# Sigmoid attention and a gated MLP on one core: in the first round the last keys' scores are placed ahead of the unit before's last values, with three smaller moves

## The chip, the core and the metric

The kernel runs on one core of a Trainium2 chip. The metric is the device time of one execution in microseconds (us); lower is better. The engines that matter here are TensorE (PE in the profile, its weight loads PEld), VectorE (DVE), ScalarE (ACT) and the queue that issues the transfers (SP). Each engine takes its instructions in the order in which the program has them; an instruction that has to wait for another engine holds back everything behind it on its own engine.

## What is computed

```python
scores = scale * np.matmul(q, k.transpose(0, 1, 3, 2)) - np.log(S)   # 8 batches, 12 heads, S = 448, head size 64
attn = 1.0 / (1.0 + np.exp(-scores))                                 # sigmoid, no row sum
x = heads side by side of np.matmul(attn, v)                         # (8, 448, 768)

h = np.maximum(x @ w_in, 0.0)                                        # (8, 448, 1024), halves u and v
v_n = (v - mean) / sqrt(var + 1e-6)                                  # over the features
v_s = einsum('ts,bsd->btd', w_spatial, v_n) + b_spatial
out = (u * v_s) @ w_out
```

All of it is in 32-bit numbers. Most products are made as three reduced-precision products of a high and a low part (`TERMS`, line 240): the high part of an operand is a rounded copy, the low part is what the copy left over. So an operand costs one cast and one subtraction before TensorE can use it.

## The kernel before

The eight batches go in four rounds of two. A round is attention for two batches, then the MLP for them: gate values (`pv`), the spatial product (`pg`), the other half (`pu`), the output (`po`). Rounds two to four use `attention` (lines 582 to 687). The first round has a routine of its own, `first_attention` (lines 528 to 580), since the weights are still being loaded and converted during it. The change is in that routine and in two helpers that it calls.

**A unit.** The first round has six units, n = 0, 2, 4, 6, 8, 10. Each holds two pairs of heads, `units[n]` and `units[n + 1]`. A pair's 448 keys are three full tiles of 128 and a rest of 64. The score tiles of a unit are numbered t: 0, 1, 2 are the full tiles of the first pair (`FIRST`), 4, 5, 6 those of the second (`SECOND`), and t = 3 is the short tile with the last 64 keys of both pairs. For each t, `attention_scores` (line 245) puts the scores of two heads into `psc`, a pair of PSUM banks, by six matmuls for a full tile (line 269) or by four plain 32-bit ones for the short tile (line 257; the profile counts each of these as two). ScalarE then writes the sigmoid into an SBUF buffer `at` (line 277). `attention_values` (line 284) multiplies the `at` tiles with the values and sums them over all seven t in one PSUM pair, `pav` (line 307). `attention_sums` (line 316) takes the finished `pav` out of PSUM as high and low parts of `x_s`: ScalarE casts the first head pair's half (line 319), VectorE casts the other half (line 320) and then makes both subtractions (line 322). In the profile's rows `qks` is a pair's split queries and keys, and `raw` what was loaded for it.

**Banks.** PSUM is used as four bank pairs, and `latest` holds them in the order of their last use. For each unit after the first they are named y, z, w, x (line 571). The short tile gets y, the full tiles get z, w, y, x, z, w, and `pav` gets y. Bank pair x still holds the `pav` of the unit before when a unit begins; t = 4, the fourth full tile, is the first to write into it. So t = 4 can begin only when all four instructions of `attention_sums` for the unit before have ended.

**Order of a unit (lines 571 to 579).** First `short_values(n - 2)`: the last products of the unit before, and its sums. Then `short_scores(n, y)`, then six full score tiles. Between some of these `load_weights(1)` runs one portion of the weight preparation (`weight_steps`, line 150). A portion is the integer part, the shift part or the split of one weight block, on VectorE; the first portion of a block also issues the transfer for the block two further on. Then come `splits(n + 2)`, a portion, `splits(n + 3)`: the high and low parts of the next unit's queries and keys, cast by ScalarE and subtracted by VectorE. Last come the products of the six full tiles. The short tile's products wait for the next unit.

**Buffers.** `at` tiles take their buffer from the list `big` of seven in turn (`slot`, line 113).

The profile's times below are of unit 2 (from 15.68 us), the others being alike.

Of the kernel before, what the change touches and what calls it, by code (L numbers as in the profile page):

```python
# [14 lines left out]
P = 128  # L15
# [20 lines left out]
def attn_gmlp_kernel(  # L36
# [25 lines left out]
    nc = tc.nc  # L62
# [9 lines left out]
    NFULL = 3  # L72

    FULL = NFULL * P
    GAP = 16
    REST = FULL + GAP
    PART = REST + S
# [28 lines left out]
    def split(hi, lo, src, copy):  # L106
        copy(hi, src)  # L107
        nc.vector.tensor_sub(lo, src, hi.bitcast(F32))  # L108

    tmp = [f"tmp_{i}" for i in range(3)]  # L110
    big = [f"big_{i}" for i in range(7)]

    def slot(tags, name, shape=(P, 2, 512), dtype=F32):
        tag = tags.pop(0)
        tags.append(tag)
        return work.tile(list(shape), dtype, tag=tag, name=name, bufs=1)

    def banks(name, tag=None):
        tag = tag or latest[0]
        latest.remove(tag)  # L120
        latest.append(tag)
        return sums.tile([P, 2, 512], F32, tag=tag, name=name)
# [71 lines left out]
    def load_weights(n):  # L194
        for _ in range(n):
            next(weights, None)
# [27 lines left out]
    def attention_splits(b, hp):  # L224
        raw = loaded[b, hp][:, HALF:]
        s = work.tile([P, 2, 2 * S], F32R, tag="split", name=f"qks_{b}_{hp}", bufs=3)
        if b == hp == 0:

            chunk, rest, query = slice(FULL - P, FULL), slice(0, FULL - P), slice(REST, PART)
            nc.vector.tensor_copy(s[:, 0, query], raw[:, query])  # L230
            for cols in (chunk, rest):
                nc.scalar.copy(s[:, 0, cols], raw[:, cols])
            for cols in (chunk, query, rest):
                nc.vector.tensor_sub(s[:, 1, cols], raw[:, cols], s[:, 0, cols].bitcast(F32))
        else:
            scalar = b == 1 or b == 0 and hp not in (1, 2)
            split(s[:, 0, :PART], s[:, 1, :PART], raw[:, :PART], nc.scalar.copy if scalar else nc.vector.tensor_copy)
        parts_of[b, hp] = s
# [6 lines left out]
    def attention_scores(b, hp, t, tag=None, slots=big, raws=None):  # L245

        psc = banks(f"psc_{b}_{hp}_{t}", tag)
        heads = [slice(j * D, (j + 1) * D) for j in range(2)]
        if t == NFULL:
            for odd in range(2):  # L250
                if raws is None:
                    raw = loaded[b, hp + odd]
                    key, query = raw[:, :HALF], raw[:, HALF + REST :]
                else:
                    key, query = raws[:, odd, :HALF], raws[:, odd, HALF:]
                for j, rows in enumerate(heads):
                    nc.tensor.matmul(  # L257
                        psc[odd * HALF : (odd + 1) * HALF, j, :S],
                        key[rows],
                        query[rows],  # L260
                        start=True,
                        stop=True,
                    )
        else:
            s = parts_of[b, hp + t // (NFULL + 1)]
            k = (t % (NFULL + 1) + NFULL - 1) % NFULL * P
            for i, (a, e) in enumerate(TERMS):
                for j, rows in enumerate(heads):
                    nc.tensor.matmul(  # L269
                        psc[:, j, :S],  # L270
                        s[rows, a, k : k + P],
                        s[rows, e, REST:PART],
                        start=i == 0,
                        stop=i == len(TERMS) - 1,
                    )
        at = slot(slots, f"at_{b}_{hp}_{t}")[:, :, :S]
        nc.scalar.activation(at, psc[:, :, :S], AF.Sigmoid, bias=bias_s, scale=QK)  # L277
        return at
# [5 lines left out]
    def attention_values(b, hp, t, at, tag=None, apart=False):  # L284

        key = b, hp, apart and t == NFULL
        if key not in pav_of:
            pav_of[key] = banks(f"pav_{b}_{hp}_{t}", tag)
            tag_of[key] = latest[-1]
        pav = pav_of[key]  # L290
        if t == NFULL and b > 1:
            latest.sort(key=lambda tag: tag == tag_of[key])
        vt = values[b, hp]
        for odd in range(2):
            if t == NFULL:
                rows = slice(odd * HALF, (odd + 1) * HALF)
            elif (t > NFULL) == odd:
                rows = slice(0, P)
            else:
                continue  # L300
            unit = key, odd
            count[unit] = count.get(unit, 0) + 1
            total = NFULL + 1 if not apart else 1 if t == NFULL else NFULL
            start, stop = count[unit] == 1, count[unit] == total
            for j in range(2):
                heads = slice(j * D, (j + 1) * D)
                nc.tensor.matmul(  # L307
                    pav[heads, odd, :S], vt[rows, t, heads], at[rows, j], start=start, stop=stop
                )
        return pav[:, :, :S]  # L310

    def x_parts(b, hp):
        x = x_s[:, :, hp : hp + 2, (b % 2) * S : (b % 2 + 1) * S]
        return x[:, 0], x[:, 1]

    def attention_sums(b, hp, pav):

        hi, lo = x_parts(b, hp)
        nc.scalar.copy(hi[:, 0], pav[:, 0])
        nc.vector.tensor_copy(hi[:, 1], pav[:, 1])  # L320
        for i in range(2):
            nc.vector.tensor_sub(lo[:, i], pav[:, i], hi[:, i].bitcast(F32))

    def product(ps, pairs, more=(), start=True, stop=True):
# [177 lines left out]
    units = [(b, hp) for b in range(B) for hp in range(NHP)]  # L502
# [21 lines left out]
    def loads(f, n, end=end):  # L524
        if n < end:
            f(*units[n])

    def first_attention():

        shorts = {}  # L530

        def splits(n):
            loads(attention_splits, n)

        def short_scores(n, tag):
            shorts[n] = attention_scores(*units[n], NFULL, tag)
            loads(attention_loads, n + 4)

        def short_values(n):
            pav = attention_values(*units[n], NFULL, shorts.pop(n))  # L540
            attention_sums(*units[n], pav)

        splits(0)
        for n in range(0, end, 2):
            unit = units[n]
            full = []

            def scores(t, tag=None):
                if n == 0 and t in (1, NFULL + 1):
                    splits(1 if t == 1 else 2)  # L550
                full.append((*unit, t, attention_scores(*unit, t, tag)))
                if t == 0:
                    loads(attention_loads, n + 3)
                    loads(value_loads, n + 2)
                if t > NFULL if n == 0 else t not in (2, TILES - 1):
                    load_weights(1)

            def products(tag=None):
                for args in full:
                    attention_values(*args, tag)  # L560

            if n == 0:
                for t in FIRST:
                    scores(t)
                short_scores(n, None)
                for t in SECOND:
                    scores(t)
                splits(3)
                products()
                continue  # L570
            y, z, w, x = latest
            short_values(n - 2)
            short_scores(n, y)
            for t, tag in zip((*FIRST, *SECOND), (z, w, y, x, z, w)):
                scores(t, tag)
            splits(n + 2)
            load_weights(1)
            splits(n + 3)
            products(y)
        short_values(end - 2)  # L580

    def attention(m):

# [11 lines left out]
        def splits(*ns):  # L595
            for n in ns:
                attention_splits(*units[first + n])
# [107 lines left out]
    for m in range(B // 2):  # L705
        if m == 0:
            first_attention()
        else:
            for _ in running:
                pass  # L710
# [87 lines left out]
```

## Time and profile before

| | |
|---|---|
| three runs | 670.29, 670.58, 670.66 us; median 670.58 us |
| the profiled execution | 670.48 us, of which the profile's span is 668.7 us |
| busy in the span | PE 664.5 us, DVE 331.2, ACT 224.8, POOL 19.4 |
| first round's attention | the span's start to 67.36 us |
| each later round | 164.6 us, of which attention 60.6 us in round two |

The span runs from the first to the last instruction that was recorded; the execution's own time has 1.8 us around it. Rows of the timeline give start, duration, engine, line, operation, tiles and shape, and in brackets the idle time of the engine before it with what ended that. Rows of the chain give start, duration and what the chain of the work that ended last went through. A weight load's (PEld) idle time shows when TensorE was held by another engine, since a matmul's recorded duration may cover a short wait.

### The profile page before, as it was taken

The numbers are of one execution on the slowest core, as the hardware profiler recorded it, in microseconds if no ns is written. First come the engines' busy times: TensorE is split into PE (matmuls) and PEld (weight loads), VectorE is DVE, ScalarE is ACT, GpSimd is POOL, SyncE is SP. The second block draws the span as 40 slices with busy tenths as digits, with TensorE's granted clock in tenths as the row PEclk, the third lists the DMA queues.
The fourth block names the chain that finished last, engine by engine and source line by source line (L and its number), as shares of the span: only waits on it lengthen the run. The fifth ranks groups of instructions, "written<-read, shape, count | busy, mean of one in ns | idle before, by whom it ended". The sixth has DMA issues, their size and how long they took to land.

```text
span 668.7 us, 9073 instructions
## 1 busy us (share of the span) xinstructions
PE 664.5 (99%) x3866; PEld 510.4 (76%) x3866; DVE 331.2 (50%) x501; ACT 224.8 (34%) x265; POOL 19.4 (3%) x36
## 2 busy tenths in 40 slices
PE   9999999999999999999999999999999999999998
PEld 5554889999655588999964558899985556899997
DVE  5999899841357447231145644722024554653201
ACT  6877010121567510002176731010128663101112
POOL 0000010000000002000000001100000000110000
PEclk9999999999999999999999999999999999999999
DMA  8783222331445300002153430000216410000022
GB/s 299 266 270 124 63 63 67 109 111 52 163 150 168 112 1 1 0 1 82 56 182 105 163 112 1 0 1 1 82 56 197 140 60 1 0 1 1 0 83 82
DMA packets 22328, 57.34 MB, mean 86 GB/s; under 512 B 2832, under 2 KB 10128, under 8 KB 22288
## 3 DMA queue, kind: packets, MB, share of 16 engines
q1 hardware_dynamic: 22288, 56.76, 25.1%
q8 instruction: 30, 0.49, 0.3%
q14 instruction: 10, 0.08, 0.0%
HBM read 45.74 MB, written 11.01 MB: 85 GB/s over the span
## 4 chain that ended last, share of the span: by engine, by line
PE 99%; DVE 0%; issue 0%
PE pav L307 20%; PE pv L328 17%; PE pu L328 17%; PE po L328 17%; PE psc L269 14%; PE pg L328 11%; PE psc L257 3%; PE idle L701 1%; PE po_end L328 0%; DVE osb L499 0%
## 5 line engine op out<-in xcount | busy, mean ns | idle before, releaser
L277 ACT ACTIVATE at<-psc,bias_s 128x896 f32<-128x896 f32 x168 | 154.3, 1017 | 44.8 <-PE psc L269 23.5
L307 PE MATMUL pav<-at,v 128*64 128x448 f32 (+1 forms) x768 | 134.6, 545 | 0.1
L328 PE MATMUL pu<-x_s,w_u_s 128*128 128x448 f32 x576 | 117.1, 362 | 0.0
L328 PE MATMUL po<-gs,w_out_s 128*128 128x448 f32 (+1 forms) x576 | 116.2, 361 | 0.0
L328 PE MATMUL pv<-w_v_s,x_s 128*128 128x512 f32 x504 | 115.5, 390 | 0.0
L328 PEld LDWEIGHTS pu<-x_s,w_u_s 128*128 128x128 f32 x576 | 108.0, 187 | 7.2
L328 PEld LDWEIGHTS po<-gs,w_out_s 128*128 128x128 f32 x576 | 107.6, 187 | 7.1
L328 PEld LDWEIGHTS pv<-w_v_s,x_s 128*128 128x128 f32 x504 | 94.3, 188 | 22.4 <-issue 2.8
L307 PEld LDWEIGHTS pav<-at,v 128*64 128x64 f32 (+1 forms) x768 | 45.4, 135 | 77.2 <-issue 57.5
L269 PEld LDWEIGHTS psc<-qks 64*128 64x128 f32 x864 | 78.6, 185 | 24.6 <-issue 6.3
L269 PE MATMUL psc<-qks 64*128 64x448 f32 x864 | 95.2, 370 | 0.1
L107 ACT CAST gs<-g 128x896 fp32r<-128x896 f32 x16 | 15.1, 941 | 182.0 <-DVE g L431 182.0
L328 PE MATMUL pg<-w_sp_s,vn 128*128 128x448 f32 x352 | 71.7, 362 | 0.0
L328 PEld LDWEIGHTS pg<-w_sp_s,vn 128*128 128x128 f32 x352 | 66.0, 187 | 4.6
L431 DVE SCALAR_TENSOR_TENSOR g<-pu,g 128x896 f32<-128x896 f32 x16 | 17.4, 1090 | 87.2 <-PE pu L328 87.2
L107 DVE CAST qks<-raw 128x848 fp32r<-128x848 f32 x38 | 22.7, 597 | 62.7 <-PE po L328 58.7
L348 ACT ACTIVATE rv<-pv 128x1024 f32<-128x1024 f32 (+1 forms) x16 | 14.7, 921 | 108.4 <-PE pv L328 108.4
L613 DVE COPY whole<-pav 128x896 f32<-128x896 f32 x15 | 16.4, 1092 | 69.9 <-PE pav L307 69.9
L108 DVE TENSOR_TENSOR qks<-raw,qks 128x848 fp32r<-128x848 f32 x47 | 49.0, 1042 | 3.8 <-ACT qks L107 2.5
L475 ACT COPY osb<-po 128x896 f32<-128x896 f32 x23 | 20.9, 907 | 75.9 <-PE po L328 75.9
L352 DVE BATCH_NORM_STATS2 stats<-rv 128x6 f32<-128x512 f32 x28 | 19.0, 678 | 31.5 <-ACT rv L348 31.5
L408 DVE TENSOR_TENSOR g<-pg,b_bc 128x896 f32<-128x896 f32 x16 | 17.4, 1088 | 19.2 <-PE pg L328 19.2
(52 smaller groups left out, 276.9 us busy)
## 6 DMA issues: line engine op xcount, KB each, us to landing
raw<-qk_dram SPq DMA_DIRECT2D x47, 456.0 KB, 4.1
v<-v_dram SPq DMA_DIRECT2D x23, 448.0 KB, 5.6
out_dram<-osb SPq DMA_DIRECT2D x23, 448.0 KB, 2.6
wraw<-w_in_dram SPq DMA_DIRECT2D x12, 512.0 KB, 4.8
wraw<-w_out_dram SPq DMA_DIRECT2D x6, 512.0 KB, 3.5
last<-qk_dram SPq DMA_DIRECT2D x3, 448.0 KB, 4.7
wraw<-w_sp_dram SPq DMA_DIRECT2D x4, 256.0 KB, 4.3
raw<-qk_dram SPq DMA_DIRECT2D x1, 296.0 KB, 2.9
```

The costliest lines, as they stand in the source:

```text
L107: copy(hi, src)
L108: nc.vector.tensor_sub(lo, src, hi.bitcast(F32))
L257: nc.tensor.matmul(psc[odd * HALF : (odd + 1) * HALF, j, :S], key[rows], query[rows], start=True, stop=True,)
L269: nc.tensor.matmul(psc[:, j, :S], s[rows, a, k : k + P], s[rows, e, REST:PART], start=i == 0, stop=i == len(TERMS) - 1,)
L277: nc.scalar.activation(at, psc[:, :, :S], AF.Sigmoid, bias=bias_s, scale=QK)
L307: nc.tensor.matmul(pav[heads, odd, :S], vt[rows, t, heads], at[rows, j], start=start, stop=stop)
L328: nc.tensor.matmul(ps, st, mv, start=start and i == 0, stop=stop and i == len(ops) - 1)
L352: nc.vector.bn_stats(stats, rv[:, i])
L408: nc.vector.tensor_add(g, pg[:, :, :S], bb)
L431: nc.vector.scalar_tensor_tensor(g, pu[:, :, :S], 0.0, g, op0=ALU.max, op1=ALU.mult)
L475: nc.scalar.copy(osb, whole_of.pop(es)[:, :, :S])
L613: copy(whole, pav)
```

## The change

Four things are changed, all for the first round alone, except that the order of the two subtractions is written in the helper `attention_sums`, which only the first round calls.

1. **Order of the short tile.** `short_scores(n)` now stands ahead of `short_values(n - 2)`. Since the `at` buffer of the unit before's short tile is then still unread when the new one is taken, the short tile's buffer is taken out of `big` (`big.pop()`) and put back when its values are done.
2. **Order of the subtractions.** `attention_sums` subtracts for the second half first.
3. **A weight portion.** The portion between `splits(n + 2)` and `splits(n + 3)` goes. In its place one runs right behind `short_values(n - 2)`, from the third unit on, and one after the last unit's sums.
4. **Second pair of the first unit.** The split of (0, 1) is made in two portions of columns: the key tile for t = 4 with the queries (592 columns), then the other two key tiles (256 columns).

```diff
@@ attention_splits
+        elif b == 0 and hp == 1:
+
+            for cols in (slice(FULL - P, PART), slice(0, FULL - P)):
+                split(s[:, 0, cols], s[:, 1, cols], raw[:, cols], nc.vector.tensor_copy)
@@ attention_sums
-        for i in range(2):
+        for i in (1, 0):
             nc.vector.tensor_sub(lo[:, i], pav[:, i], hi[:, i].bitcast(F32))
@@ first_attention
         def short_scores(n, tag):
-            shorts[n] = attention_scores(*units[n], NFULL, tag)
+            at = attention_scores(*units[n], NFULL, tag)
+            shorts[n] = big.pop(), at
             loads(attention_loads, n + 4)
 
         def short_values(n):
-            pav = attention_values(*units[n], NFULL, shorts.pop(n))
+            slot_of, at = shorts.pop(n)
+            pav = attention_values(*units[n], NFULL, at)
+            big.append(slot_of)
             attention_sums(*units[n], pav)
@@
             y, z, w, x = latest
+            short_scores(n, y)
             short_values(n - 2)
-            short_scores(n, y)
+            if n > 2:
+                load_weights(1)
             for t, tag in zip((*FIRST, *SECOND), (z, w, y, x, z, w)):
                 scores(t, tag)
             splits(n + 2)
-            load_weights(1)
             splits(n + 3)
             products(y)
         short_values(end - 2)
+        load_weights(1)
```

What that does to ScalarE's order at the start of unit 2, first as it was (in a name such as `at_2_3_241` the 2 is the unit, the 3 is t, the last number only a count; lines of the new kernel stand 4 further down here):

```order
L107 CAST qks_3_212<-raw_3_138 128x848
L319 CAST x_s<-pav_0_0_215 128x448
L277 ACTIVATE at_2_3_241<-psc_2_3_236,bias_s 128x2x448
L277 ACTIVATE at_2_0_252<-psc_2_0_245,bias_s 128x2x448
L277 ACTIVATE at_2_1_270<-psc_2_1_263,bias_s 128x2x448
```

And ScalarE at the same place now:

```order
L107 CAST qks_3_214<-raw_3_138 128x848
L281 ACTIVATE at_2_3_235<-psc_2_3_230,bias_s 128x2x448
L323 CAST x_s<-pav_0_0_217 128x448
L281 ACTIVATE at_2_0_254<-psc_2_0_247,bias_s 128x2x448
L281 ACTIVATE at_2_1_272<-psc_2_1_265,bias_s 128x2x448
```

The short tile's sigmoid and the cast of unit 0's `pav` have changed places, since ScalarE follows the order in which the code is written.

VectorE from the end of unit 2 into unit 4, as it was:

```order
L108 TENSOR_TENSOR qks_4_318<-raw_4_170,qks_4_318 128x848
L107 CAST w_sp_s<-wraw_258 128x512
L108 TENSOR_TENSOR w_sp_s<-wraw_258,w_sp_s 128x512
L108 TENSOR_TENSOR qks_5_325<-raw_5_254,qks_5_325 128x848
L320 CAST x_s<-pav_2_0_328 128x448
L322 TENSOR_TENSOR x_s<-pav_2_0_328,x_s 128x448 x2
```

And VectorE at the same place now:

```order
L108 TENSOR_TENSOR qks_4_320<-raw_4_172,qks_4_320 128x848
L108 TENSOR_TENSOR qks_5_323<-raw_5_256,qks_5_323 128x848
L324 CAST x_s<-pav_2_0_326 128x448
L326 TENSOR_TENSOR x_s<-pav_2_0_326,x_s 128x448 x2
L107 CAST w_sp_s<-wraw_260 128x512
L108 TENSOR_TENSOR w_sp_s<-wraw_260,w_sp_s 128x512
```

The weight portion has moved from between the two splits to behind the sums. On TensorE the eight short score matmuls and the eight short value matmuls (as the profile counts them) change places; both stand between the last full products and the first full score tile, before and now.

## The prediction

> **What bounds the kernel now.** I read the page first, then the chain of work that ended last, since it shows which engine a saving has to be made on.
>
> ```profile
> span 668.7 us, 9073 instructions
> ...
> PE 664.5 (99%) x3866; PEld 510.4 (76%) x3866; DVE 331.2 (50%) x501; ACT 224.8 (34%) x265; POOL 19.4 (3%) x36
> ...
> PE 99%; DVE 0%; issue 0%
> ```
>
> TensorE is the chain from beginning to end. What it gains or loses in the first round goes into the time one for one, since no later stage has idle time in which a delay could vanish. So I went to the chain in the first round, piece by piece: start, duration, matmuls.
>
> ```profile
> 15.68 0.75 PE psc L257 x8
> 16.43 3.91 PE psc L269 x36
> ...
> 26.74 3.92 PE psc L269 x36
> ...
> 37.05 4.05 PE psc L269 x36
> ...
> 47.43 4.05 PE psc L269 x36
> ...
> 57.80 3.98 PE psc L269 x36
> ```
>
> These five are the full score tiles of units 2 to 10, 36 matmuls each. A stage of the second round shows what the same 36 take undisturbed:
>
> ```profile
> 191.73 3.81 PE psc L269 x36
> ```
>
> So the units lose 0.10, 0.11, 0.24, 0.24 and 0.17 us, together 0.86 us. That is all that a better order can win in units 2 to 10. The waits in the window of the first round name who held the score tiles' weight loads:
>
> ```profile
> PEld psc L269 <- ACT at L277: 1.6, 6, 0.7
> PEld psc L269 <- DVE x_s L322: 0.7, 3, 0.3
> ```
>
> The first is t = 2 waiting for bank pair y, until the short tile's sigmoid has read it. The second is t = 4 waiting for bank pair x, until the sums of the unit before have left it.
>
> **The change, part by part: the order of the short tile.** This part decides. The timeline of unit 2 has all its links:
>
> ```profile
> 15.75 0.53 ACT L319 CAST x_s<-pav 128x448 fp32r<-128x448 f32 x1 [1.68 <-PE pav L307]
> 16.32 0.62 DVE L320 CAST x_s<-pav 128x448 fp32r<-128x448 f32 x1 [1.12 <-ACT x_s L319]
> 16.36 3.98 PE L269 MATMUL psc<-qks 64*128 64x448 f32 x36
> 16.59 6.41 ACT L277 ACTIVATE at<-psc,bias_s 128x896 f32<-128x896 f32 x7 [0.31 <-PE psc L257]
> 16.86 1.15 DVE L322 TENSOR_TENSOR x_s<-pav,x_s 128x448 fp32r<-128x448 f32 x2
> 17.65 2.32 PEld L269 LDWEIGHTS psc<-qks 64*128 64x128 f32 x24 [0.18 <-ACT at L277]
> 17.92 0.42 DVE L107 CAST w_sp_s<-wraw 128x512 fp32r<-128x512 f32 x1
> 18.37 0.69 DVE L108 TENSOR_TENSOR w_sp_s<-wraw,w_sp_s 128x512 fp32r<-128x512 f32 x1
> ```
>
> Before, `pav` was finished at 15.68. ScalarE was free and began its cast 0.07 later; VectorE's cast began at 16.32, 0.04 after ScalarE's had ended (15.75 + 0.53 = 16.28), having sat idle for it; both subtractions were done at 16.86 + 1.15 = 18.01, before t = 4 wanted x. Only then came the short sigmoid, at 16.59, and t = 2 was held a little for it.
>
> Now the two short groups change places on TensorE, and neither becomes longer by it, so the full tiles still begin at 16.36. The new links, with the durations of the rows:
>
> - The short scores end where the short values ended, 15.68. The sigmoid followed their end (15.68 + 0.75 = 16.43) by 0.16, so it begins at 15.84.
> - Seven sigmoids of 1.02 take 6.41, so one follows another by (6.41 - 1.02) / 6 = 0.90. ScalarE's cast, behind the first of them, begins at 16.74. Its input is there at 16.43 + 0.07 = 16.50; it is the sigmoid ahead of it that makes it late. It ends at 17.27.
> - VectorE's cast waits for it: 17.31 to 17.93.
> - The subtraction that is now first reads what this cast has written, so it must wait for it; before, it read ScalarE's and started 0.08 before the cast's end (16.86 against 16.94). A dependent pair stands in the last two rows: 18.37 is 0.03 after 17.92 + 0.42. So the two run from 17.96 to 19.11.
>
> When does t = 4 want bank x? Half of an undisturbed group, and the mean of one matmul:
>
> ```profile
> 191.66 2.08 PE L269 MATMUL psc<-qks 64*128 64x448 f32 x18
> ```
> ```profile
> L269 PE MATMUL psc<-qks 64*128 64x448 f32 x864 | 95.2, 370 | 0.1
> ```
>
> The last pair of 18 starts 2.08 - 0.37 = 1.71 after the first; pairs follow each other by about 0.20 (36 matmuls in 3.81), so the nineteenth starts 1.91 after the first: 16.36 + 1.91 = 18.27. How fast TensorE resumes, and what a held tile costs besides, I take from unit 6, where x already came late:
>
> ```profile
> 36.34 1.03 DVE L108 TENSOR_TENSOR qks<-raw,qks 128x848 fp32r<-128x848 f32 x1
> 36.37 0.53 ACT L319 CAST x_s<-pav 128x448 fp32r<-128x448 f32 x1 [1.48 <-PE pav L307]
> 36.98 2.92 PE L269 MATMUL psc<-qks 64*128 64x448 f32 x24
> 37.29 0.62 DVE L320 CAST x_s<-pav 128x448 fp32r<-128x448 f32 x1
> 37.83 1.14 DVE L322 TENSOR_TENSOR x_s<-pav,x_s 128x448 fp32r<-128x448 f32 x2
> 39.02 0.70 PEld L269 LDWEIGHTS psc<-qks 64*128 64x128 f32 x8 [0.25 <-DVE x_s L322]
> ```
>
> The loads go on 0.05 after the subtractions end (38.97). Without bank x, t = 4 would have begun at 36.98 + 1.91 + 0.10 (the sigmoid's stall, as in unit 2) = 38.99, so it was only 0.03 late; yet the unit lost 0.24. The remaining 0.24 - 0.10 - 0.03 = 0.11 is what a restart costs.
>
> So t = 4 begins at 19.11 + 0.05 = 19.16 instead of 18.27: 0.89 late, with the restart 1.00. The short sigmoid's stall is gone (it ends at 15.84 + 1.02 = 16.86; t = 2 wants y after twelve matmuls, at about 17.65). ScalarE's chain behind is no later than before: the first full tile's sigmoid began at 16.59 + 0.90 = 17.49, and the cast ends at 17.27. The stage becomes 3.81 + 1.00 = 4.81 in each unit, and all five are alike, since VectorE is now held by ScalarE's cast and no longer by its own work. Five times 4.81 is 24.05; before it was 3.91 + 3.92 + 4.05 + 4.05 + 3.98 = 19.91. **Cost: 4.14 us.**
>
> A rule of the Trainium skill speaks about one link. "VectorE: DVE Perf Modes", section "The DRAIN you can't avoid", says that a semaphore between two VectorE instructions costs nothing extra; the pairs above differ by 0.11 with the wait and without, and the sum goes by the rows. By the rule, five units would lose about 0.55 less.
>
> **The order of the subtractions** alone wins nothing: t = 4 needs both, and both stand behind VectorE's cast. Its price is the 0.11 a unit counted above.
>
> **The weight portion.** In unit 6 VectorE was still in a split until 36.34 + 1.03 = 37.37 while ScalarE's cast had ended at 36.90: that is why units 6 to 10 lost more than units 2 and 4. With the portion gone from between the splits, VectorE is free in time, but it now waits for the later cast, so this win (in the 0.86) is covered. The portion's own work stays: it runs behind the sums, under the score tiles. Whether VectorE still fits shows in the two windows of one unit, with the columns PE, PEld, DVE:
>
> ```profile
> 30.66:36.30 5.64, 5.64 (x36) 2.14 (x40) 4.78 (x9) 4.22 (x5) 0.00 (x0) 1.00 0.66 205
> 36.30:41.11 4.81, 4.81 (x47) 3.21 (x40) 4.71 (x9) 4.44 (x6) 0.00 (x0) 1.00 0.86 308
> ```
>
> 9.49 of 10.45 us are busy; 1.8 of it are the sums, the rest, 7.7, now begins when they end, 2.75 after the score tiles' start, and is over at about 10.5. The longer unit lasts 11.3, and the next sums come 0.95 after that: nothing is late, with 1.7 us to spare. Transfers on SP's queue change places with this portion (a weight load with a load of queries and keys), but VectorE waited only 0.3 us for weights in the whole round; I put this at nothing, and at up to 0.5 us if a load comes late. The portion after the last sums pushes VectorE by about 1.2 us in the MLP. What TensorE needs from there first:
>
> ```profile
> 91.46 0.75 DVE L370 SCALAR_TENSOR_TENSOR vn<-rv,rstd,vn 64x512 fp32r<-64x512 f32 x1
> ...
> 100.04 0.69 DVE L108 TENSOR_TENSOR w_u_s<-wval,w_u_s 128x512 fp32r<-128x512 f32 x1
> ```
> ```profile
> 96.15 8.80 PE pg L328 x44
> 104.95 14.40 PE pu L328 x72
> ```
>
> Both are ready 3.9 to 4.2 us ahead, so this costs nothing.
>
> **The buffers.** The short tile takes the buffer released first, and the unit's last full tile the one that the short values have just left. No sigmoid waits for a reader that is still to come: nothing.
>
> **The second pair of unit 0.**
>
> ```profile
> 6.50 0.60 DVE L107 CAST qks<-raw 128x848 fp32r<-128x848 f32 x1 [1.33 <-DMA raw<-qk_dram]
> 7.14 1.04 DVE L108 TENSOR_TENSOR qks<-raw,qks 128x848 fp32r<-128x848 f32 x1
> 7.89 2.22 PE L269 MATMUL psc<-qks 64*128 64x448 f32 x18
> 8.23 1.50 PEld L269 LDWEIGHTS psc<-qks 64*128 64x128 f32 x16 [0.16 <-DVE qks L108]
> ```
>
> The 18 matmuls take 2.22 against 2.08 undisturbed: 0.14 lost, since t = 4 waits for the low part until 8.18. For 592 columns I estimate a cast of 0.46 and a subtraction of 0.78, between the rows of 512 (0.42, 0.69) and 848 columns: done at 7.77, well ahead. The other columns follow by about 8.5; t = 5 wants them at about 8.7. **Gain: 0.14 us**, between 0 and 0.14.
>
> **Sum.** 670.48 + 4.14 - 0.14 = 674.5 us for an execution like the profiled one; the median of the runs lies 0.1 above it, within the rounding of the links. Predicted: 674.5.
>
> **The rivals.** *The sums are not held (faster).* VectorE's cast would start when `pav` is complete, at 16.50, and not wait for ScalarE's. Then it and the first subtraction run to about 17.8, the second follows ScalarE's cast, x is free near 18.3, and the stalls go: 670.5 - 0.86 - 0.14 = 669.5. The point from which it decides is a cast that starts before about 16.6. For it speaks that the two casts read different halves, and that the swapped subtractions suit it. The Trainium skill, "PSUM — Partial Sum Buffer", section on bank collisions, asks for a guard between two engines only where they share a bank, and the halves are banks of their own. Against it stands the row of unit 2: VectorE sat idle 1.12 us until ScalarE's cast was done. Chance 0.06.
>
> *No net change.* The portion's move and the earlier sigmoid win about as much as the later sums lose, if x comes only 0.2 late, at 18.5 (0.2 a unit, with no restart, is 1.0, against the 0.86 + 0.14 won). That needs the cast to go ahead of the sigmoid, but ScalarE has them in the other order: 670.6, chance 0.04.
>
> *The dependent subtraction costs nothing.* Five times 0.11 less: 673.9, chance 0.15, still slower.
>
> *VectorE falls behind.* If transfers or the weight work delay the splits by 0.2 in each unit: 675.5, chance 0.10, slower.
>
> **How the numbers follow.** The forecast has the remaining 0.65. What is slower adds up to 0.90. The range goes from 672.6 (no extra wait, no restart cost: 674.5 - 0.55 - 0.55, and three quarters of a us for rounding in five units) to 675.7 (VectorE behind, and nothing won in unit 0). It leaves out the two rivals of 0.10. About 0.2% is what a measurement of this kernel can tell from no change.
>
> **What would show it.** In the profile after: ScalarE's cast at L323 right behind a sigmoid, VectorE's cast idle until it ends, t = 4's loads held by L326 for most of a us in five units, the five score stages at about 4.8 us, the first unit's 18 matmuls at 2.08. Score stages at or under 3.9 would prove me wrong.

## The result and the profile after

| | before | after |
|---|---|---|
| median of six runs each | 670.62 us (670.14 to 671.09) | 674.57 us (674.20 to 675.04) |
| the profiled execution | 670.48 us, span 668.7 | 674.36 us, span 672.5 |

The ratio is 1.006, with a 95% interval of 1.0047 to 1.0073: the change costs 3.95 us, between 3.15 and 4.9. The forecast was 674.5. One of the four executions of experiment 2 below took 1724.33 us, for which nothing on record gives a reason, and is left out of its ratio. In the code after, the lines of the profile stand four further down: the score tiles are L273 (short ones L261), the products L311, the sigmoids L281, the sums L323, L324 and L326.

On the page, TensorE has lost its hold on the chain:

```profile
PE 97%; DVE 1%; ACT 1%; issue 0%; ACTq 0%
```

The 2% that now belong to other engines all lie in the first round. The chain of after in unit 2, piece by piece (start, duration, what):

```profile
14.15 0.98 PE psc L261 x8
...
15.21 1.01 ACT at L281
16.22 0.43 ACT x_s L323
...
16.68 0.64 DVE x_s L324
17.34 1.17 DVE x_s L326 x2
18.50 0.14 issue
18.64 2.08 PE psc L273 x18
20.72 4.66 PE pav L311 x24
```

It reads as the new path of bank pair x: the short scores, their sigmoid, ScalarE's cast of the sums behind it, VectorE's cast behind that, two subtractions, and only then t = 4 with the second 18 matmuls. Before, this stretch was one unbroken piece of TensorE. The same path stands in every unit, at a fixed distance; the products of unit 4, and those of unit 10, three units on:

```profile
31.95 4.66 PE pav L311 x24
...
65.65 5.57 PE pav L311 x32
```

From one unit's products to the next it takes 11.23 us (31.95 - 20.72, and a third of 65.65 - 31.95). The same distance before is best read from the short scores, of which the first, at 15.68, stands in the prediction (the last row is the first MLP matmul):

```profile
25.99 0.75 PE psc L257 x8
...
36.30 0.75 PE psc L257 x8
...
46.68 0.75 PE psc L257 x8
...
57.05 0.75 PE psc L257 x8
...
67.36 2.72 PE pv L328 x11
```

These are 10.31, 10.31, 10.38, 10.37 and 10.31, together 51.68 us; after, the five are 56.16, by the starts of the products in the chain (unit 0's at 9.49, unit 10's at 65.65). So units 2 to 10 lose 4.48 us. The waits of after in the first round (total, times, longest) name the two links that are new:

```profile
DVE x_s L324 <- ACT x_s L323: 9.7, 6, 2.5
...
PE psc L273 <- DVE x_s L326: 4.1, 5, 0.8
```

TensorE's 0.8 for the subtractions, five times, is most of the loss; VectorE in turn waits for ScalarE's cast. The timeline of unit 2 has the starts:

```profile
15.74 2.08 PE L273 MATMUL psc<-qks 64*128 64x448 f32 x18
16.12 0.53 ACT L323 CAST x_s<-pav 128x448 fp32r<-128x448 f32 x1
16.68 0.62 DVE L324 CAST x_s<-pav 128x448 fp32r<-128x448 f32 x1 [1.83 <-ACT x_s L323]
...
18.61 1.74 PEld L273 LDWEIGHTS psc<-qks 64*128 64x128 f32 x18 [1.17 <-PE psc L273]
18.64 2.08 PE L273 MATMUL psc<-qks 64*128 64x448 f32 x18 [0.82 <-DVE x_s L326]
```

The first full score starts at 15.74. Counted from there, the sigmoid begins at -0.53 (15.21 in the chain), ScalarE's cast at 0.38, VectorE's at 0.94; the subtractions end (18.50 in the chain) at 2.76 and t = 4 begins at 2.90. Undisturbed it would begin at 1.91.

One other thing differs, in unit 0. Before:

```profile
4.22 2.83 PE psc L269 x17
...
7.96 2.15 PE psc L269 x18
```

and after:

```profile
4.18 2.38 PE psc L273 x18
...
7.47 2.01 PE psc L273 x18
```

The second pair's 18 went from 2.15 to 2.01, which is the split in portions (0.14). The first 18 went from 2.83 to 2.38, and nothing in the change touches them. For the two profiled executions the account is then 4.48 - 0.14 - 0.45 = 3.89 us; their times differ by 3.88.

### The profile page after: what moved, and what is told of

Same layout as the page of the kernel before. It is cut to its first block, busy times and chain, and to the rows that moved or that the text cites. A ratio compares the mean times of both kernels' runs of the same rounds, so it can differ in the third digit from the quotient of the medians.

```text
span 672.5 us, 9077 instructions
## 1 busy us (share of the span) xinstructions
PE 664.3 (99%) x3866; PEld 511.0 (76%) x3866; DVE 332.2 (49%) x503; ACT 225.3 (34%) x265; POOL 19.4 (3%) x36
## 4 chain that ended last, share of the span: by engine, by line
PE 97%; DVE 1%; ACT 1%; issue 0%; ACTq 0%
PE pav L311 19%; PE pv L332 17%; PE pu L332 17%; PE po L332 17%; PE psc L273 12%; PE pg L332 10%; PE psc L261 3%; DVE x_s L326 1%; ACT at L281 1%; PE idle L710 0%; DVE x_s L324 0%; ACT x_s L323 0%; PE po_end L332 0%; DVE osb L503 0%; ACTq L281 0%
## 5 line engine op out<-in xcount | busy, mean ns | idle before, releaser
L281 ACT ACTIVATE at<-psc,bias_s 128x896 f32<-128x896 f32 x168 | 155.4, 1014 | 55.3 <-PE psc L261 31.1
L311 PE MATMUL pav<-at,v 128*64 128x448 f32 (+1 forms) x768 | 134.7, 543 | 0.1
L311 PEld LDWEIGHTS pav<-at,v 128*64 128x64 f32 (+1 forms) x768 | 45.9, 136 | 75.8 <-issue 56.2
L273 PEld LDWEIGHTS psc<-qks 64*128 64x128 f32 x864 | 79.2, 185 | 28.0 <-issue 9.2
L273 PE MATMUL psc<-qks 64*128 64x448 f32 x864 | 95.2, 368 | 4.1 <-DVE x_s L326 4.1
L107 DVE CAST qks<-raw 128x848 fp32r<-128x848 f32 (+2 forms) x39 | 22.8, 586 | 61.0 <-PE po L332 57.6
L108 DVE TENSOR_TENSOR qks<-raw,qks 128x848 fp32r<-128x848 f32 (+2 forms) x48 | 48.8, 1023 | 1.3
```

What stands on the lines that cost most here:

```text
L273: nc.tensor.matmul(psc[:, j, :S], s[rows, a, k : k + P], s[rows, e, REST:PART], start=i == 0, stop=i == len(TERMS) - 1,)
L311: nc.tensor.matmul(pav[heads, odd, :S], vt[rows, t, heads], at[rows, j], start=start, stop=stop)
```

## The experiments

The theory: the time is lost by the new order alone, since it finishes the values 0.75 us later and puts a sigmoid ahead of ScalarE's cast, and the sums are one chain of four instructions behind that cast. The rivals: the moved weight portion or the transfers cost something too, or the swapped subtractions do; and, for a way out, that VectorE's cast could go ahead on its own half.

In each, "pitch" is the distance from one unit's full products to the next unit's. Each kernel is compared with before, run on the same chip.

**1. The order put back, all else as in the change.**

```diff
             y, z, w, x = latest
-            short_scores(n, y)
             short_values(n - 2)
+            short_scores(n, y)
```

> The changed kernel with only the order of the short tile put back: short values first, then short scores; the other three parts stay. Theory (the order of the short tile is the whole loss): the sums end about 0.9 us earlier against the score tiles, bank x is free before t = 4 asks for it in all five units, only the 0.1 us stall for the short sigmoid stays, so a unit's pitch (start of its full products to start of the next unit's) falls from 11.23 to about 10.31 us and the time to 670.2 us (670.6 less 0.14 for unit 0 and about 0.15 for units 6 and 8, where VectorE was late). Rival (the moved weight portion and the transfers that change places with it cost part of the loss): pitch above 10.5 in some units, time over 671.5 us.

Measured: 670.24 us (669.84 to 670.77), ratio 0.9996 [0.9987, 1.0004]. The chain of this kernel, the score stages of units 2 and 6:

```profile
16.53 3.90 PE psc L273 x36
...
37.14 3.90 PE psc L273 x36
```

The pitch is 10.30 or 10.31 in all five units (half of 37.14 - 16.53), unit 6 takes 3.90 where it took 4.05, and the two that took 10.38 and 10.37 before have come down to it too. So all of the loss is the order's. The other three parts together win 0.15 in the five units (51.53 in place of 51.68). In unit 0 this profile shows no gain, since the second pair's data came late (experiment 8). That is too little to show in the time.

**2. The order alone, on the kernel before.**

```diff
+            at = attention_scores(*units[n], NFULL, tag)
+            shorts[n] = big.pop(), at
...
+            big.append(slot_of)
...
+            short_scores(n, y)
             short_values(n - 2)
-            short_scores(n, y)
```

> The kernel before with only the order of the short tile changed (short scores first, with its buffer handling); the subtractions, the weight portion and unit 0's split as before. Theory: the loss is there in full but for the dependent subtraction, which has its old order again: pitch 11.23 - 0.11 = 11.12 us in each unit, time about 670.6 + 5 x 0.78 = 674.5 us (no gain in unit 0). Rival (the weight portion takes part in the loss): pitch clearly under 11 us and time under 673 us.

Measured: 674.38 us, ratio 1.0057 [1.0042, 1.0073]. Its chain in unit 2:

```profile
17.97 1.07 DVE x_s L322 x2
19.04 0.14 issue
...
21.25 4.66 PE pav L307 x24
...
32.35 4.66 PE pav L307 x24
```

The path is that of after and the pitch 11.10. Here the subtraction that comes first is the one of ScalarE's half, and the two take 1.07 of the chain and not 1.17.

**3. After, with the old order of the subtractions.**

```diff
-        for i in (1, 0):
+        for i in range(2):
```

> The changed kernel with only the order of the two subtractions put back (first half first). Theory (the subtraction now first waits for the write of the cast ahead of it, 0.11 us): the subtractions follow the cast with an overlap again, bank x is free 0.11 us earlier, pitch 11.12 instead of 11.23 us, time about 674.0 us. Rival (a wait between two VectorE instructions costs nothing extra): pitch 11.23 us, time 674.6 us.

Measured: 674.15 us, ratio 1.0052 [1.0037, 1.0068], pitch 11.10. The timeline of this kernel in unit 2:

```profile
17.65 0.62 DVE L324 CAST x_s<-pav 128x448 fp32r<-128x448 f32 x1 [2.37 <-ACT x_s L323]
18.19 1.15 DVE L326 TENSOR_TENSOR x_s<-pav,x_s 128x448 fp32r<-128x448 f32 x2
```

The first subtraction starts at 18.19, 0.08 before the cast has ended (17.65 + 0.62 = 18.27). In after it starts 0.04 behind the cast's end (17.34 against 17.30), since it reads what that cast wrote. With the pitch of 11.23 beside 11.10, the dependent pair costs 0.13 us a unit. The rule of the Trainium skill, "VectorE: DVE Perf Modes", section "The DRAIN you can't avoid", that a semaphore between two VectorE instructions costs nothing extra, does not hold here. The same page's section "Two Vector instructions with no wait between them", by which only a held instruction has to wait until every earlier one on VectorE has finished, agrees with the 0.08.

**4. After, with VectorE's cast ahead of ScalarE's.**

```diff
+        nc.vector.tensor_copy(hi[:, 1], pav[:, 1])
         nc.scalar.copy(hi[:, 0], pav[:, 0])
-        nc.vector.tensor_copy(hi[:, 1], pav[:, 1])
```

> The changed kernel with VectorE's cast of the second half issued ahead of ScalarE's cast of the first half, so that VectorE's no longer waits for ScalarE's and ScalarE's waits for VectorE's instead. All else as in the change. Theory (t = 4 waits at the end of a chain: sigmoid, ScalarE cast, VectorE cast, subtractions): counted from the first full score matmul, VectorE's cast runs from 0.14 to 0.76, ScalarE's from 0.79 to 1.32, the subtractions end at about 1.97, t = 4 begins near 2.1 instead of 2.9; pitch about 10.45 us, time about 671.1 us. Rival (x is late because the short values are finished 0.75 us later, whatever the casts do): pitch stays at 11 us or more, time at 673.5 us or more.

Measured: 673.67 us, ratio 1.0046 [1.0033, 1.006], pitch 11.00. The main expectation missed by 0.55 us a unit, and the numbers are those of the rival. The chain of this kernel in unit 2, and below it a line of its timeline:

```profile
16.53 0.64 DVE x_s L323
...
17.18 0.54 ACT x_s L324
```

```profile
17.75 1.16 DVE L326 TENSOR_TENSOR x_s<-pav,x_s 128x448 fp32r<-128x448 f32 x2 [0.60 <-ACT x_s L324]
```

VectorE's cast does start right behind the values, no longer behind the sigmoid. But ScalarE's cast now waits for VectorE's, and the first subtraction, which is of VectorE's own half, waits 0.60 us for ScalarE's. Both casts write the one tile `x_s` and read the one tile `pav`, and the four instructions stay a chain in both orders. That the waits stand there because of the shared tiles is read from the program; no run gives the halves tiles of their own. Only the sigmoid has gone from in front of it, and that is worth 0.23.

**5. After, with the sums' cast ahead of the sigmoid.** The short scores' matmuls stay ahead of the short values; only the sigmoid is issued behind the sums. (`attention_scores` with `later=True` hands the sigmoid back to be issued later; the diff here has only the call.)

```diff
-            short_scores(n, y)
+            sigmoid = attention_scores(*unit, NFULL, y, later=True)
+            loads(attention_loads, n + 4)
             short_values(n - 2)
+            at = sigmoid()
+            shorts[n] = big.pop(), at
```

> The changed kernel, TensorE's order as changed, but ScalarE takes its cast of the unit before's sums ahead of the short tile's sigmoid. Theory (most of the lateness is that the short values end 0.75 us later; the sigmoid ahead of the cast adds only about 0.24): counted from the first full score matmul, the cast begins at 0.14 instead of 0.38, t = 4 begins at about 2.66 instead of 2.90, t = 2 now waits for the sigmoid until about 1.65; pitch 11.0 us, time about 673.4 us. Rival (the sigmoid ahead of the cast is the whole cause): t = 4 begins near 2.0, pitch 10.3 us, time about 670.5 us.

Measured: 673.87 us, ratio 1.0052 [1.0035, 1.0069], pitch 11.00. Its chain in unit 2 shows two holds instead of one:

```profile
16.53 0.53 ACT x_s L326
17.06 0.92 ACT at L282
...
18.02 0.90 PE psc L273 x6
...
21.13 4.66 PE pav L314 x24
...
32.13 4.66 PE pav L314 x24
```

t = 2 is held by the late sigmoid until 18.02. The sums, which follow the cast as before, end at the same moment as t = 2, as the timeline shows (17.75 + 1.16 = 18.91):

```profile
17.75 1.16 DVE L329 TENSOR_TENSOR x_s<-pav,x_s 128x448 fp32r<-128x448 f32 x2
```

t = 4 begins 0.14 later, again 0.23 earlier in its unit than in after. So the sigmoid ahead of the cast is the smaller part of the lateness. The larger one is that the values themselves finish 0.75 us later, which no order of ScalarE mends.

**6. After, with the sums on VectorE alone,** one cast and one subtraction for both halves.

```diff
-        nc.scalar.copy(hi[:, 0], pav[:, 0])
-        nc.vector.tensor_copy(hi[:, 1], pav[:, 1])
-        for i in (1, 0):
-            nc.vector.tensor_sub(lo[:, i], pav[:, i], hi[:, i].bitcast(F32))
+        nc.vector.tensor_copy(hi, pav)
+        nc.vector.tensor_sub(lo, pav, hi.bitcast(F32))
```

> The changed kernel with the sums of a unit made by VectorE alone: one cast and one subtraction over both halves, none on ScalarE. Theory (the length of the chain behind the values decides, from 0.14 after the first full score matmul): a cast of 1.09, 0.03, a subtraction of 1.09, 0.14 until the loads resume: t = 4 at about 2.5 instead of 2.90, pitch about 10.83 us, time about 672.6 us; still slower than before, because the values end too late for any chain of over 1.7 us. Rival (the hand-over between ScalarE and VectorE is what costs): pitch under 10.5 us, time under 671.2 us.

Measured: 672.99 us, ratio 1.0038 [1.0025, 1.0051], pitch 10.83. The chain in unit 2:

```profile
16.74 1.10 DVE x_s L323
...
17.87 1.10 DVE x_s L324
...
21.18 4.66 PE pav L311 x24
...
32.02 4.66 PE pav L311 x24
```

Without ScalarE the path from the values' end to t = 4 is 1.10 + 1.10 and three gaps, and 0.40 us of each unit come back. Even so the order costs 0.5 us a unit. The sums begin 0.14 after the first full score (16.60 in the timeline) and end 2.36 after it, while undisturbed t = 4 would want bank x at 1.91. Sums short enough to fit were not tried.

**7. The weight portion alone, on the kernel before.**

```diff
             short_scores(n, y)
+            if n > 2:
+                load_weights(1)
...
             splits(n + 2)
-            load_weights(1)
             splits(n + 3)
...
         short_values(end - 2)
+        load_weights(1)
```

> The kernel before with only the weight portion moved. Theory: VectorE is free when ScalarE's cast ends, so the sums end 1.64 after the first full score matmul in all units (before: up to 1.99 in units 6 and 8), pitch 10.31 us in all five, units 6 and 8 lose 0.07 us less; time 670.3 us. Rival (the moved transfers make the splits late): pitch above 10.4 us in some unit.

Measured: 670.31 us in one execution, and pitches of 10.30 or 10.31 in all five units. In unit 6, where before ScalarE's cast had ended at 36.90 and VectorE's began only at 37.29, the timeline now has

```profile
36.94 0.62 DVE L320 CAST x_s<-pav 128x448 fp32r<-128x448 f32 x1 [0.69 <-ACT x_s L319]
```

VectorE is there before ScalarE and waits 0.69. This shows that the portion between the splits was what made units 6 and 8 longer, and that moving it is worth 0.15 us in all (51.53 in place of 51.68).

**8. The second pair's split alone, on the kernel before.**

```diff
+        elif b == 0 and hp == 1:
+            for cols in (slice(FULL - P, PART), slice(0, FULL - P)):
+                split(s[:, 0, cols], s[:, 1, cols], raw[:, cols], nc.vector.tensor_copy)
```

> The kernel before with only the second pair of unit 0 split in two portions. Theory: if the pair's data land as early as in the profile of before, the second 18 matmuls of unit 0 and the start of the full products come 2.01 us apart instead of 2.15; if they land 0.4 us later, about 2.3. Units 2 to 10 as before, pitch 10.31 to 10.38 us; time within 0.5 us of before, which one execution cannot tell. Rival (the two portions delay VectorE's split for unit 2): a later start of unit 2's score tiles, pitch of unit 0 over 10.5 us.

Measured: 670.60 us in one execution. The chain of its second pair, and the timeline of the first portion:

```profile
8.08 2.16 PE psc L273 x18
```

```profile
6.97 0.47 DVE L107 CAST qks<-raw 128x592 fp32r<-128x592 f32 x1 [1.82 <-DMA raw<-qk_dram]
7.47 0.78 DVE L108 TENSOR_TENSOR qks<-raw,qks 128x592 fp32r<-128x592 f32 x1
```

Here the pair's data landed at 6.97, 1.04 ahead of the first matmul of t = 4 (8.01 in the timeline); in the profiled execution of before the distance was 1.39, in that of after 1.41. The low part is ready at 8.25, t = 4 still waits for it, and 2.16 is no better than the 2.15 of before. But in before the data came earlier. A like case without the split is the profile of experiment 2: there the data landed 1.08 ahead, and from the first matmul of t = 4 to the products it took 2.46. So with data as late as here the portions win about 0.3, by one profile each, more than the 0.14 that they win where the data come early. In experiments 1, 4, 5 and 6 the data landed 0.92 ahead, and with the split the stretch took 2.28 or 2.29.

**9. A wait less for the short sigmoid, on the kernel of experiment 1.** There the sigmoid waits for TensorE and, for its buffer, for ScalarE's own earlier work. A copy of one element, issued after the last full sigmoid of a unit, makes that second wait unnecessary; later rounds have the same line. It also stands behind unit 0's last sigmoid (not shown).

```diff
+            nc.scalar.copy(mark, full[-1][-1][:1, 0, :1])
             splits(n + 2)
             splits(n + 3)
```

> The kernel of the first experiment (short values first, the other three parts of the change kept), with one small addition: behind the six full tiles' sigmoids ScalarE copies one element of the last one into the unused tile mark. That copy waits for ScalarE's own earlier writes, so the next unit's short sigmoid waits for TensorE alone and no longer for two semaphores. Theory (what still holds the score tiles by 0.10 us a unit is t = 2 waiting for the short sigmoid, and that sigmoid's start carries about 0.09 us for its second wait): the short sigmoid starts 0.13 instead of 0.22 us after the first full score matmul, t = 2 is no longer held, pitch about 10.20 us in place of 10.31, time about 669.7 us, below both kernels. Rival (the 0.10 us is the score tiles' own, or the second wait costs nothing): pitch 10.30 us, time 670.2 us.

Measured: 670.07 us (669.31 to 670.30), ratio 0.9989 [0.998, 0.9998]. This is the one version that beats the kernel before, by 0.1% (0.02 to 0.2%). The waits of the first round, of the kernel of experiment 1:

```profile
ACT at L281 <- PE psc L261: 1.5, 5, 0.3
...
PEld psc L273 <- ACT at L281: 1.6, 6, 0.7
```

and of this one:

```profile
PEld psc L273 <- ACT at L281: 0.7, 1, 0.7
...
ACT at L281 <- PE psc L261: 1.2, 5, 0.2
```

The sigmoid starts 0.06 us earlier in each of five units, and t = 2 is no longer held by it. The trace shows why: in experiment 1 a semaphore instruction (one that only waits, and is not counted as busy) starts on ScalarE 0.06 us ahead of each of these five sigmoids, and here it is gone. The chain has score stages of 3.84 to 3.86 where they were 3.90 to 3.92:

```profile
16.39 3.84 PE psc L273 x36
...
20.24 5.64 PE pav L311 x32
...
30.48 5.64 PE pav L311 x32
```

The pitch is 10.25. It was expected to be 10.20: the second wait cost 0.06 and not 0.09, and about 0.05 a unit above the undisturbed 10.20 (3.81 + 5.64 + 0.75) is left, of which no row says what it is.

## Why the prediction was right

**The links.** In unit 2, counted from the first full score, the sigmoid was put at -0.52 and measured at -0.53; ScalarE's cast at 0.38 and 0.38; VectorE's at 0.95 and 0.94; the end of the subtractions at 2.75 and 2.76. The rows of before carried them all.

**How TensorE resumes.** Forecast 0.05 after the subtractions' end, from unit 6 of before; measured 0.14, in after and in each of experiments 2 to 6. (The 0.05 was to the weight load; counted so, after has 0.11, from 18.50 to 18.61, and the first matmul follows 0.03 later.) The restart cost behind it was forecast at 0.11 and is 0.04: an undisturbed unit is 3.81 of scores, 5.64 of products and 0.75 of short scores, 10.20; after's 11.23 is 1.03 above it, and t = 4 was 0.99 late. The two errors cancel to 0.03 a unit. The traces show what differs. In unit 6 of before the load itself waits for VectorE. In after, and in experiments 2 to 6, a semaphore instruction of 0.05 us waits for VectorE first, and the load behind it waits for TensorE's own earlier work. The length of the stop does not set it: from the last matmul's start to the next one's it is 0.51 us in experiment 5 and 1.18 in after, and TensorE resumes 0.14 to 0.15 after the subtractions in all of them. The prediction counted one wait where the new order has two.

**What the stalls before were worth.** This term was too large: 0.86 us by the chain's pieces, 0.68 by the pitches (51.68 less five times 10.20). The chain's piece of 4.05 in unit 6 is followed by products of 5.57, the piece of 3.92 by 5.64: where TensorE had been held, the border of the pieces lies 0.07 later. So 0.24 was 0.17. With the stage 0.03 longer than forecast, five units lose 4.48 and not 4.14.

**Unit 0.** The split won 0.14 in the profiled execution, as forecast. Its upper bound of 0.14 holds only for data that come as early as there; where they are later, it wins about 0.3 (experiment 8). What balanced the units' extra 0.34 there is the 0.45 by which the first 18 matmuls were faster, and that is chance, below. For the medians, 4.48 - 0.14 = 4.34 stands beside 3.95, inside the interval. That the forecast lies only 0.1 from the median is partly luck: the account of the units was 0.3 short.

**The weight portion, the buffers and the end** were put at nothing, and experiment 1 shows them at that: with the order put back the pitch is 10.31 and the time that of before. Under the new order the portion costs nothing either: experiment 2, which doesn't move it, and experiment 3, which does, both have a pitch of 11.10.

**The rivals.** *The sums are not held*: VectorE's cast waited 1.83 us for ScalarE's, and experiment 4 shows that where it goes first, the first subtraction waits for ScalarE all the same. *No net change* needed x only 0.2 late; it was 0.85 late. *The dependent subtraction costs nothing*: it costs 0.13 a unit, by experiment 3. *VectorE falls behind*: it waits for ScalarE in all five units, so it was never late itself.

## What to carry to other kernels

When two groups change places on a busy engine, follow the one that moved back: whatever hangs on its result is later by the other group's whole length (here 0.75 us), plus what now stands ahead of its first reader on that reader's engine (0.23), and it costs nothing only as long as the next use of its buffer is further away than that. Before counting on two engines to share a job by halves, look in the trace whether they ever ran side by side; here four instructions on two halves of one tile were a chain in every order that was run. Read a stage's length from start to start over several stages, since the border between two pieces of a chain can move by as much as the stall that one is looking for.

## What was not expected of the hardware

**A second wait has a price.** ScalarE's short sigmoid starts 0.06 us earlier when one of its two waits is taken away (experiment 9). TensorE's weight load follows VectorE's subtractions by 0.11 us where it has a second wait (after), by 0.05 where it has one (unit 6 of before).

**The start of TensorE.** The first 18 score matmuls of unit 0 took 2.38 us in after, 2.83 in before and 2.97 in experiment 8, 3.36 in experiment 3 and 3.02 in experiment 9, though all run the same 18. The chain of experiment 3, beside that of after (shown with the result):

```profile
4.18 3.36 PE psc L273 x18
```

The matmuls take 0.57 us each at first and later 0.36, and the change comes at another moment in each execution: at about 4.9 us in after, 5.8 in before and 6.9 in experiment 3. The row of the granted clock shows 9 (90% or more) in the first slices all the same. The Trainium skill, "TensorE: Matmul & The Clock Gate", Part 1, says that the clock starts low, that a free-running window of about 3.4 us decides when it rises, and that the number of slow matmuls therefore differs from run to run; the traces agree in that the moment moves, and no row here shows the clock itself change. It does not always reach the time. In experiments 4 and 6 the first 18 took only 2.34 and 2.37, but the short scores behind them waited for a transfer and took 1.49 and 1.55 in place of 0.91. Over all profiles here the products of unit 0 start between 9.49 (after) and 10.46 (experiment 3), 1 us apart, a quarter of the effect that was measured.
